# Matmuls on constants in the places where the program's own clock sees TensorE wait

## The chip, the cores and the metric

The kernel runs on one core of one Trainium2 chip. The metric is the device time of one execution in microseconds (us). TensorE (PE) multiplies into PSUM, where VectorE (DVE) and ScalarE (ACT) read the results; GpSimd (POOL) splits weights and issues some DMAs, and SyncE (SP) issues most of them. PEld is TensorE's loading of weights. The kernel uses PSUM as one tile of 8 banks of 512 fp32 values in each of 128 partitions.

## The reference, cut to what matters

Four layers in a row on a sequence of 2048 rows of 512 values, with 32 heads of 16 values: layer A (attention over all keys, with one key and value head for all 32 query heads), layer B (causal attention within four segments of 512 rows and a running memory beside it), then A and B again with the same weights. `phi(t)` is `t + 1` for positive `t`, else `exp(t)`.

```python
def _A_ref(x, wq, wk, wv, wo):            # H = 32, Dh = 16
    q = (x @ wq) by heads;  k = x @ wk;  v = x @ wv
    p = _softmax(einsum("bhqd,bkd->bhqk", q, k) * Dh ** -0.5)
    return einsum("bhqk,bkd->bhqd", p, v) by rows @ wo

def _B_ref(x, wq, wk, wv, wo, beta):      # N = 4 segments of L = 512
    for s in range(N):
        p = _softmax(qs @ ks.T * scale + mask)           # causal in the segment
        a_dot = p @ vs
        a_mem = (phi(qs) @ M) / (phi(qs) @ z + 1e-6)
        o = g * a_mem + (1.0 - g) * a_dot                # g = sigmoid(beta)
        M = M + phi(ks).T @ vs;  z = z + phi(ks) summed over rows
    return o @ wo

for layer in (A, B, A, B):
    x = x + layer(_layernorm(x, axis=-1))
```

## The kernel before

The rows are cut into four blocks of 512. A pair is one layer A and the layer B behind it; there are two pairs.

Layer A's attention (`a_scores`, `a_products`) runs unit by unit: a unit is four heads of one block, and each unit goes over 16 key tiles of 128. For a key tile TensorE writes two groups of eight small score matmuls (49 rows by 32 columns, written `bank<-qa,kst`, the first of a group at L99, the others at L102), ACT turns each group into exponentials `pa` (L751), and sixteen matmul halves multiply them by the values (`bank<-pa,va`). Scores live in pairs of PSUM banks, the ring `sc`; the exponentials live in nine buffers.

Everything else is the side work of a block (`side`): the output projection of A with the norm behind it (`out_norm`, `norm_tiles`: transposes at L514, `xh` and `xl`), the inputs of B (`b_inputs`: projections at L454, `qf`, `parts`, a bounce through DRAM by DMA, `sb<-parts` and `qkb<-sb`), the row maxima of its scores (`b_rowmax` with L988, in the last block `b_rowmax_masked` with L959), a transpose of the maxima (`guard_rows`, L687), its attention (`b_attend`, exponentials at L1027) and the output projection of B. These use single banks, the ring `r`: two of them (banks 4 and 5) beside layer A, six in the last part of the preparation, eight or four in the last block.

The order of the instructions is made when the program is built. The writer keeps a clock for each engine, `clk`, and adds an estimated cost for everything it emits: `pe(cost, form)` for TensorE, where `form` is how the array is split ("full", "rows" or "cols") and a change of form adds `DRAIN` = 130 ns; `on(engine, after, cost)` for the others. Each part of the work is a generator that yields the time at which its next piece can start (a bank of its ring free, its inputs there). `weave` runs the units of A beside the side work of one block, and `step` picks the generator whose next piece starts first; if that time lies ahead of `clk["pe"]`, the clock is set forward to it. There are eight phases, 0 to 7: phase 0 is laid beside the preparation, the others beside the side work of one block each. The side work of the very last block has no units beside it: `drive` runs it alone, from about 3000 us on. `together` issues a matmul that stays behind the one before it in TensorE's order.

`idb` is the identity and `maskq` a mask, both constants in SBUF (bf16).

Of the kernel before, what the change touches and what calls it, by code (L numbers as in the profile page):

```python
# [38 lines left out]
P = 128  # L39
S, D, H, DH = 2048, 512, 32, 16  # L40
NB, BT = 4, 512
# [48 lines left out]
def net_kernel(ctx, tc, x_in, a_wq, a_wk, a_wv, a_wo, b_wq, b_wk, b_wv, b_wo, b_beta, cst, out):  # L90
# [5 lines left out]
    def together(first, *a, **k):  # L96

        if first:
            nc.tensor.matmul(*a, **k)  # L99
        else:  # L100
            with tc.high_priority(offset=400):
                tc.keep_in_program_order(nc.tensor.matmul(*a, **k))  # L102
# [45 lines left out]
    def nm(s):  # L148
        uid[0] += 1
        return f"{s}_{uid[0]}"  # L150

    def st(shape, dt, tag):
        return one.tile(shape, dt, tag=tag, name=nm(tag))
# [15 lines left out]
    clk = {"pe": 0.0, "act": 0.0, "dve": 0.0, "pool": 0.0}  # L169
    evac_on = ["dve"]  # L170
    tiling = ["full"]

    def pe(cost, form="full"):
        clk["pe"] += cost + (DRAIN if form != tiling[0] else 0.0)
        tiling[0] = form
        return clk["pe"]
# [12 lines left out]
    def load_x(b):  # L189
        r = []  # L190
        for i in range(4):
            x_ = tmp(4, [P, 512], F32, "xt")
            nc.sync.dma_start(x_, x_in[b * BT + i * P:b * BT + (i + 1) * P, :])
            r.append(x_)
        return r
# [9 lines left out]
    maskq = st([P, 512], BF16, "maskq")  # L205
# [3 lines left out]
    idb = st([P, P], BF16, "idb")  # L209
# [89 lines left out]
    def wget(kind, n, ahead=2):  # L299

        wprefetch(n)
        r = []
        for j in range(n):
            k, i, w = wq_["ready"].pop(0)
            assert k == kind, (k, kind)
            r.append(w)
        wprefetch(ahead)
        return r
# [48 lines left out]
    rings = {}  # L357

    def layout(kind):

        n = clk["pe"]
        sc, r = {"a": (3, ()), "ab": (2, (4, 5)), "b": (2, (4, 5, 6, 7)), "b0": (0, (4, 5, 6, 7, 0, 1, 2, 3)), "z": (0, (4, 5, 6, 7, 0, 1, 2, 3)), "prep": (0, (0, 1, 2, 3, 4, 5)), "pa": (2, (4, 5))}[kind]
        for k, v in (("sc", pair_[:sc]), ("r", [one_[i] for i in r])):
            rings[k] = Ring(v)
            rings[k].free = [n] * len(v)

    def drive(gen):
        for rdy in gen:
            clk["pe"] = max(clk["pe"], rdy())

    class Need:
# [11 lines left out]
    def form_of(need):  # L383
        return need.form() if isinstance(need, Need) else "full"
# [25 lines left out]
    def step(zs, cost):  # L410

        now = clk["pe"]
        best = None
        for z in zs:
            if z[1] is None:
                continue
            at = z[1]()
            s = max(now, at) + (2 * DRAIN if form_of(z[1]) != tiling[0] else 0.0) + cost(z)
            if best is None or s < best[0]:
                best = s, at, z  # L420
        s, at, z = best
        assert at < 1e17
        clk["pe"] = t0 = max(now, at)
        z[1] = next(z[0], None)
        return z, clk["pe"] - t0

# [12 lines left out]
    def finish(za, until):  # L439
        while not until() and any(z[1] is not None for z in za):  # L440
            step(za, lambda z: PVL if z is za[1] else 0.0)
# [185 lines left out]
    def a_layer(i, exact):  # L627
        qmx = tmp(2, [32, 2 * NB], F32, "qmx")
        V.memset(qmx, 0.0)
        return {"exact": exact, "kst": kst[i], "va": va[i], "kr": [1e18] * NB, "qr": [[1e18] * 4 for _ in range(NB)],  # L630
                "sd": [dram.tile([H, 48, 512] if exact else [H, 33, 512], BF16 if exact else F16, tag=nm("sd"), name=nm("sd")) for _ in range(NB)],
                "kmx": tmp(2, [P, NB], F32, "kmx"), "qmx": qmx, "part": {}, "old": {}, "nq": 0}
# [131 lines left out]
    def a_products(n):  # L764

        for _ in range(n):
            yield Need(lambda: max(queue[0][-1], pva_free[0] if queue[0][1] else 0.0) if queue else 1e18, "rows")
            a_pv(*queue.pop(0))
# [372 lines left out]
    def everything(exact):  # L1141
        xs = [x_in] + [dram.tile([S, D], F32, tag=nm("x"), name=nm("x")) for _ in range(3)] + [out]
        L = a_layer(0, exact)

        spare = [x.rearrange("p j c -> p (j c)") for x in qa]
        spare = [x.bitcast(F32R).rearrange("p (a c) -> p a c", a=2) for x in spare]
        wq_["todo"] += ([("Akv", 0)] if exact else []) + [("Aq", t) for t in range(4)]
        for pair in range(2):
            for b in range(NB):
                ws = [("Ao", t) for t in range(4)] + [("Bv", t) for t in range(4)]  # L1150
                for t in range(4):
                    ws += [("Bq", t), ("Bk", t)]
                ws += [("Bo", t) for t in range(4)]
                if pair == 1 and b >= NB - 2:
                    end = b == NB - 1
                    ws = [(k, t, spare[t] if end and k == "Bv" and t < 2 else None, "take" if end else "keep") for k, t in ws]
                wq_["todo"] += ws
                if pair == 0:
                    wq_["todo"] += [("Akv", 0)] + [("Aq", t) for t in range(4)]
        aw = wget("Akv", 1) + wget("Aq", 4, 0)  # L1160
        layout("prep")
        evac_on[0] = "act"

        def prep(bs):
            bs = list(bs)
            if 0 in bs:
                ahead[0] = load_x(0) if exact else x_0, None
            for b in bs:
                xt, st_ = ahead.pop(b)
                for tiles in ((0, 1), (2, 3)) if st_ is None else ((0, 1, 2, 3),):  # L1170
                    yield from norm_tiles(xt, tiles, clk["pe"] + LOAD, st_)
                if b < NB - 1:
                    xt = load_x(b + 1)
                    ahead[b + 1] = xt, norm_stats(xt, (0, 1, 2, 3), clk["pe"] + LOAD)
                yield from a_prep(L, b, aw, b == 0 and not exact)
                evac_on[0] = "dve"

        ahead = {}

        def units(f, L, *parts):  # L1180
            return [(L, f, b, n, k0, k1) for b, k0, k1 in parts for n in range(8)]

        def side(b, pair, L, last=False):
            yield from out_norm(ota, 0, "Ao", xs[2 * pair], xs[2 * pair + 1], b, True, True)
            yield from b_block(b, last, exact, not exact and pair == 0 and b == 0)
            if last:
                layout("z")
            yield from out_norm(otb, 1, "Bo", xs[2 * pair + 1], xs[2 * pair + 2], b, pair == 0, False)
            if pair == 0:
                yield from a_prep(L, b, None)  # L1190

        if exact:
            drive(prep(range(NB)))
            layout("ab")
            for pair in range(2):
                LN = a_layer(1, exact)
                for b in range(NB):
                    drive(par(a_scores(units(0, L, (b, 0, 16))), a_products(128)))
                    drive(side(b, pair, LN))
                L = LN  # L1200
            return

        zb = prep(range(NB))
        while L["qr"][0][0] > 1e17:
            clk["pe"] = max(clk["pe"], next(zb)())
        layout("pa")
        LN = a_layer(1, exact)
        plan = [units(0, L, (0, 0, 4), (0, 4, 16))]
        plan += [units(f, L, (f, 0, 16)) for f in range(1, 4)]
        plan += [units(4, LN, (0, 0, 12), (1, 0, KA), (0, 12, 16)), units(5, LN, (1, KA, 16))]  # L1210
        plan += [units(f, LN, (f - 4, 0, 16)) for f in range(6, 8)]
        size = [sum(u[5] - u[4] for u in q) for q in plan]
        gone.clear()
        za = [[g, next(g)] for g in (a_scores(sum(plan, [])), a_products(sum(size)))]
        for f in range(8):
            phase[0] = f
            ta = (size[f] - gone.get(f, 0) - (32 if f == 4 else 0)) * 1500.0
            if f == 0:
                weave(za, TA0, zb, 55e3)
            else:  # L1220
                layout("ab")
                weave(za, TAF * ta, side((f - 1) % 4, (f - 1) // 4, LN), 150e3 if f < 5 else 133e3)
            layout("a")
            finish(za, lambda: gone.get(f, 0) == size[f])
            if f == 3:
                a_range(L)
        a_range(LN)
        layout("b0")
        evac_on[0] = "act"
        drive(side(NB - 1, 1, None, True))  # L1230
        assert not wq_["ready"] and not wq_["todo"]

    everything(False)
# [44 lines left out]
```

## Time and profile before

| | |
|---|---|
| median of 3 runs | 3179.75 us (3176.38 to 3182.36) |
| the profiled execution | 3173.99 us |
| its span, first to last instruction | 3172.1 us |
| mean granted TensorE clock in it | 0.975 of full |
| instructions | 116270 |

Times in the profile count from the start of the span. An engine's busy time is given in us and as a share of the span. A row of a group of instructions reads: line, engine, operation, tiles written and read, rows and columns of the array, shape, count, then busy us and mean ns of one, then the idle time just before them and what ended it. A row of a wait reads: who, for whom, us in total, times, longest. A row of the timeline reads: start, us, engine, line, and in brackets the idle time before it and its releaser. A row of the critical chain reads: start, us, engine, line. A row of a stretch has its bounds and length, the busy time of PE, PEld, DVE, ACT and POOL with instruction counts, the granted clock of TensorE (1.00 is full speed), the share of the DMA engines and GB/s.

### The profile page before, as it was taken

The numbers are of one execution on the slowest core, as the hardware profiler recorded it, in microseconds if no ns is written. First come the engines' busy times: TensorE is split into PE (matmuls) and PEld (weight loads), VectorE is DVE, ScalarE is ACT, GpSimd is POOL, SyncE is SP. The second block draws the span as 40 slices with busy tenths as digits, with TensorE's granted clock in tenths as the row PEclk, the third lists the DMA queues.
The fourth block names the chain that finished last, engine by engine and source line by source line (L and its number), as shares of the span: only waits on it lengthen the run. The fifth ranks groups of instructions, "written<-read, shape, count | busy, mean of one in ns | idle before, by whom it ended". The sixth has DMA issues, their size and how long they took to land.

```text
span 3172.1 us, 116270 instructions
## 1 busy us (share of the span) xinstructions
PE 2799.0 (88%) x51714; PEld 1329.8 (42%) x51714; DVE 1656.8 (52%) x4599; ACT 2325.2 (73%) x2583; POOL 396.0 (12%) x569
## 2 busy tenths in 40 slices
PE   6988898899888998889998898988998889988987
PEld 4533344345333454434443343443443334433544
DVE  7621355545655456556465454565445535555465
ACT  4699787876778767787778768668687876878523
POOL 2100010012100121002110020210110003100011
PEclk9999999999999999999999999999999999999978
DMA  4310121012210132102221132311221104311331
GB/s 124 99 42 22 46 63 43 25 50 78 67 39 18 54 91 58 35 15 73 89 63 46 33 108 66 92 47 34 84 63 31 48 12 160 95 48 33 114 106 34
DMA packets 138560, 194.11 MB, mean 61 GB/s; under 512 B 29664, under 2 KB 97088, under 8 KB 138048
## 3 DMA queue, kind: packets, MB, share of 16 engines
q1 hardware_dynamic: 118912, 121.56, 13.1%
q0 software_dynamic: 19136, 65.02, 7.2%
q8 instruction: 407, 6.67, 0.9%
q14 instruction: 105, 0.86, 0.1%
HBM read 126.46 MB, written 60.03 MB: 59 GB/s over the span
## 4 chain that ended last, share of the span: by engine, by line
PE 38%; ACT 31%; issue 15%; DVE 10%; DMA 3%; POOL 2%; SPq 0%; DVEq 0%; ACTq 0%; POOLq 0%
ACT pa L751 28%; PE bank L99 16%; PE bank L454 13%; PE bank L102 7%; DVE mo L988 4%; ACT pa L1027 3%; DVE m L959 1%; POOL w L186 1%; POOL parts L550 1%; DMA xt<-in_A_x_dram 1%; DMA wst<-in_B_wk_dram 1%; PE bank L514 1%; DMA wst<-in_B_wq_dram 1%; DVE parts L552 0%; DVE qf L532 0%
## 5 line engine op out<-in xcount | busy, mean ns | idle before, releaser
L751 ACT ACTIVATE pa<-bank 128x1024 f32<-128x1024 f32 x2048 | 1945.1, 1113 | 470.0 <-PE bank L102 465.5
L102 PE MATMUL bank<-pa,va 64*17 64x512 f32 x14336 | 1107.4, 601 | 0.2 <-DVE t L790 0.2
L99 PE MATMUL bank<-pa,va 64*17 64x512 f32 x2048 | 1065.5, 601 | 15.8 <-DVE ts L789 9.2
L99 PE MATMUL bank<-qa,kst 49*32 49x512 f16 x2048 | 746.1, 383 | 179.4 <-ACT pa L751 150.3
L102 PE MATMUL bank<-qa,kst 49*32 49x512 f16 x14336 | 827.9, 388 | 0.6 <-DVE xt L835 0.6
L988 DVE CUSTOM_DVE_ANT_0 mo<-bank,maskq 128x256 bf16<-128x256 f32 (+3 forms) x896 | 437.9, 489 | 209.5 <-PE bank L102 145.0
L102 PEld LDWEIGHTS <-kst 49*32 49x32 f16 x14336 | 227.5, 90 | 509.5 <-issue 498.7
L99 PE MATMUL bank<-qkb 48*32 48x128 f16 (+7 forms) x1536 | 346.4, 311 | 104.4 <-DVE m L988 46.0
L1027 ACT ACTIVATE pa<-bank 128x1024 f32<-128x1024 f32 (+2 forms) x384 | 323.7, 887 | 127.5 <-PE bank L102 125.1
L102 PE MATMUL bank<-qkb 48*32 48x384 f16 (+7 forms) x6656 | 369.9, 313 | 0.0
L99 PEld LDWEIGHTS <-kst 49*32 49x32 f16 x2048 | 174.3, 92 | 364.9 <-issue 340.3
L454 PE MATMUL bank<-xh,w 128*128 128x512 f32 x832 | 286.7, 409 | 11.6 <-DVE w L318 4.8
L102 PEld LDWEIGHTS bank<-pa,va 64*17 64x17 f32 x14336 | 259.4, 95 | 24.7 <-DVE t L790 8.8
L186 POOL TENSOR_SCALAR w<-wst 128x512 fp32r<-128x512 f32 x160 | 108.4, 679 | 1189.5 <-PE bank L454 1033.3
L454 PE MATMUL bank<-w,xh 128*128 128x512 f32 x752 | 246.7, 408 | 2.5 <-DVE xh L825 1.1
L102 PEld LDWEIGHTS <-qkb 48*32 48x32 f16 (+1 forms) x6656 | 152.8, 94 | 211.6 <-issue 202.6
L99 PEld LDWEIGHTS bank<-pa,va 64*17 64x17 f32 x2048 | 186.7, 94 | 105.7 <-DVE ts L789 14.5
L789 DVE STREAM_TRANSPOSE ts<-bank 128x512 f32<-128x512 f32 x88 | 62.8, 714 | 279.1 <-PE bank L102 278.9
L99 PEld LDWEIGHTS <-qkb 48*32 48x32 f16 (+1 forms) x1536 | 130.1, 96 | 155.0 <-issue 124.5
L454 PEld LDWEIGHTS bank<-xh,w 128*128 128x128 f32 x832 | 158.7, 191 | 80.0 <-issue 30.9
L1038 DVE STREAM_TRANSPOSE t<-bank 128x512 f32<-128x512 f32 x64 | 45.8, 715 | 273.6 <-PE bank L102 273.6
L102 PE MATMUL bank<-pa,vb 128*17 128x384 f32 (+3 forms) x1920 | 171.4, 442 | 8.5 <-ACT pa L1027 7.6
(164 smaller groups left out, 2987.5 us busy)
## 6 DMA issues: line engine op xcount, KB each, us to landing
sb<-parts SPq DMA_DIRECT2D x128, 128.0 KB
qkb<-sb SPq DMA_DIRECT2D x256, 64.0 KB
x<-xt SPq DMA_DIRECT2D x48, 256.0 KB
xt<-x SPq DMA_DIRECT2D x48, 256.0 KB
qa<-sd SPq DMA_DIRECT2D x176, 66.0 KB
wd<-w POOLq DMA_DIRECT2D x20, 512.0 KB, 3.7
w<-wd POOLq DMA_DIRECT2D x18, 512.0 KB, 6.1
xt<-in_A_x_dram SPq DMA_DIRECT2D x32, 256.0 KB
```

The source lines that it names most:

```text
L99: nc.tensor.matmul(*a, **k)
L102: tc.keep_in_program_order(nc.tensor.matmul(*a, **k))
L186: G.tensor_scalar(o, i, 1.0, 0.0, op0=ALU.mult, op1=ALU.add)
L454: T.matmul(ps, lhsT=l_(kt), rhs=r_(kt), start=n == 0, stop=n == 11)
L514: T.transpose(ps[:, k, :], xn[:, k * P:(k + 1) * P], ident)
L550: G.tensor_scalar(parts[:, 0, :], x, up, 0.0, op0=ALU.mult, op1=ALU.add)
L751: A.activation(x, sc, AF.Exp, scale=scale)
L789: V.transpose(ts.rearrange("p a b -> p (a b)"), pva[:, 0, :])
L959: V.reduce_max(m[:, u0:u0 + per, i, qt], ps[:, 0:per * nk].rearrange("p (h k) -> p h k", k=nk), axis=AX.X)
L988: V.tensor_tensor_reduce(out=mo[:, 0:nk], in0=ps[:, o_:o_ + nk], in1=maskq[:, 512 - nk:512], op0=ALU.add, op1=ALU.max, scale=1.0, scalar=- ...
L1027: A.activation(e[:, :, 0:w], sc[:, :, 0:w], AF.Exp, scale=0.25 if exact else 0.25 / (UPB * UPB))
L1038: V.transpose(t1.rearrange("p a b -> p (a b)"), pvb)
```

## The change

`fill(until)` is new. Where `step` would set TensorE's clock forward to `at`, and, in the side work of the last block, before each yielded time, it writes matmuls on constants: identity (`idb`) against `maskq`, into the bank of the ring `r` that was freed first. It does so only while more than 400 ns of the wait are left, less than 0.7 of the last 3400 ns on TensorE's clock is booked as work, and a bank of the ring is free by the clock. A matmul has up to 512 moving columns; it uses all 128 columns of the array if the current form is "full", and 32 of them otherwise. What they write is never read. `busy` is the list of booked work for that share. The matmuls count on `clk["pe"]` with their cost and with `DRAIN`, so the choices of `step` after them can differ too.

```diff
+    SPAN = 3400.0
+    DUTY = 0.7
+    busy = []
+
+    def duty():
+        while busy and busy[0][1] < clk["pe"] - SPAN:
+            busy.pop(0)
+        return sum(b - max(a, clk["pe"] - SPAN) for a, b in busy) / SPAN
+
+    def fill(until):
+
+        ring = rings["r"] if rings["r"].slots else None
+        while ring and until - clk["pe"] > 400.0 and duty() < DUTY and min(ring.free) < clk["pe"]:
+            i = min(range(len(ring.free)), key=lambda j: ring.free[j])
+            rows, cols_ = (P, P) if tiling[0] == "full" else (P, 32)
+            n = int(min(512, max(128, (until - clk["pe"] - 260.0) * 2.4))) // 64 * 64
+            together(False, ring.slots[i][0:cols_, 0:n], lhsT=idb[0:rows, 0:cols_], rhs=maskq[0:rows, 0:n], start=True, stop=True)
+            pe(n / 2.4, "cols" if cols_ == 32 else "full")
+
     def pe(cost, form="full"):
+        busy.append((clk["pe"], clk["pe"] + cost))
...
-    def drive(gen):
+    def drive(gen, warm=False):
         for rdy in gen:
+            if warm:
+                fill(rdy())
             clk["pe"] = max(clk["pe"], rdy())
...
         s, at, z = best
         assert at < 1e17
-        clk["pe"] = t0 = max(now, at)
+        fill(at)
+        clk["pe"] = t0 = max(clk["pe"], at)
         z[1] = next(z[0], None)
         return z, clk["pe"] - t0
...
-        drive(side(NB - 1, 1, None, True))
+        drive(side(NB - 1, 1, None, True), True)
```

In the changed program the lines behind the new functions have moved: L454 is L477, L514 is L537, L687 is L710; `together` keeps L99 and L102. The program gets 171 such matmuls, each with a load of `idb`: 133 in the phases, 38 in the last block. All other instructions are the same ones, but many stand in another order.

The first place is TensorE in phase 1 (about 464 us): the last scores of one group of eight and the first of the next. Before:

```order
L102 LDWEIGHTS kst_21_121
L102 MATMUL bank<-qa_26_130,kst_21_121 32x512
L99 LDWEIGHTS kst_21_121
L99 MATMUL bank<-qa_26_130,kst_21_121 32x512
L102 LDWEIGHTS kst_21_121
L102 MATMUL bank<-qa_26_130,kst_21_121 32x512
```

and now:

```order
L102 LDWEIGHTS kst_21_121
L102 MATMUL bank<-qa_26_130,kst_21_121 32x512
L102 LDWEIGHTS idb_97
L102 MATMUL bank<-maskq_95,idb_97 32x512
L99 LDWEIGHTS kst_21_121
L99 MATMUL bank<-qa_26_130,kst_21_121 32x512
```

One filler of 128 rows by 32 columns has come between two groups of scores; nothing else moved here.

The second place is TensorE in the last block, between the transpose of the first unit's maxima (`m`) and the first scores of the second unit, whose queries and keys are `qkb_28`. Before:

```order
L102 LDWEIGHTS idb_97
L102 MATMUL bank<-maskw_106,idb_97 32x128
L687 MATMUL bank<-cs_89,m_52850 16x128
L99 LDWEIGHTS qkb_28_132
L99 MATMUL bank<-qkb_28_132 32x512
```

and now, of six equal fillers the first:

```order
L102 LDWEIGHTS idb_97
L102 MATMUL bank<-maskw_106,idb_97 32x128
L710 MATMUL bank<-cs_89,m_52997 16x128
L102 LDWEIGHTS idb_97
L102 MATMUL bank<-maskq_95,idb_97 128x512
```

Six full fillers now stand behind the transpose and ahead of the first scores of the second unit.

The third place is TensorE a little earlier in the last block, at the transposes of the norm's third and fourth tile (`xn`). Before:

```order
L454 MATMUL bank<-w_52691,xl_157 128x512
L514 MATMUL bank<-cs_89,xn_52745 128x128 x4
L514 MATMUL bank<-cs_89,xn_52773 128x128 x4
L454 MATMUL bank<-qa_25_129,xh_156 128x512 x2
L454 MATMUL bank<-xh_156,w_52693 128x512
```

and now, behind the third tile's transposes:

```order
L477 MATMUL bank<-w_52824,xh_156 128x512 x2
L477 MATMUL bank<-w_52824,xl_157 128x512
L537 MATMUL bank<-cs_89,xn_52884 128x128 x4
L102 LDWEIGHTS idb_97
L102 MATMUL bank<-maskq_95,idb_97 128x512
```

Eight full fillers have come between the third tile's transposes and the fourth's (`xn_52912`), which ran one behind the other.

## The prediction

> **What bounds the kernel now.** I read the busy shares first, then the waits of TensorE (PE) and ScalarE (ACT), then the clock by stretch, then the last block row by row.
>
> ```profile
> PE 2799.0 (88%) x51714; PEld 1329.8 (42%) x51714; DVE 1656.8 (52%) x4599; ACT 2325.2 (73%) x2583; POOL 396.0 (12%) x569
> PE 38%; ACT 31%; issue 15%; DVE 10%; DMA 3%; POOL 2%; SPq 0%; DVEq 0%; ACTq 0%; POOLq 0%
> L99 PE MATMUL bank<-qa,kst 49*32 49x512 f16 x2048 | 746.1, 383 | 179.4 <-ACT pa L751 150.3 <-ACT pa L1027 9.3 <-DVE qmx L599 0.4
> ...
> 27.20:3000.00 2972.80, 2647.57 (x49103) 1240.69 (x49101) 1537.01 (x4295) 2269.19 (x2509) 359.33 (x505) 0.98 0.21 59
> 3000.00:3172.10 172.10, 141.31 (x2582) 81.30 (x2582) 100.09 (x242) 51.50 (x68) 25.42 (x40) 0.82 0.28 86
> ```
>
> PE is busy 88% of the span, ACT 73%, and the chain that ended last changes between them: neither covers the other. The two stretches (us, then busy time of PE, PEld, DVE, ACT, POOL, then granted clock) say what a lower clock can cost at most: in the eight interleaved phases and before, to 3000, 0.02 x 2973 = 59 us, in the last block alone 0.18 x 172 = 31 us.
>
> ```profile
> PE bank L99 <- ACT pa L751: 168.0, 451, 5.0
> PE bank L99 <- DVE m L988: 46.0, 100, 2.4
> ...
> ACT pa L751 <- PE bank L102: 465.5, 298, 10.8
> ```
>
> PE really waits for a score bank 451 times, 0.37 us each (168.0 / 451), which is 22% of the 2048 score groups that L99 begins. ACT starves for scores 298 times.
>
> **The filler in the phases.** By the instruction order 133 fillers are added there, 128 rows by 32 columns, with 61,888 moving columns in all (121 times 512), in 110 places, two thirds of them straight ahead of a score group. They stand where the bookkeeping's clock waits, not the chip's. The price of one is bounded by the nearest rows, a lone 128-row matmul between products and scores:
>
> ```profile
> 506.73 0.59 PE L99 MATMUL bank<-pa,va 64*17 64x512 f32 x1
> 506.73 0.61 PE L102 MATMUL bank<-pa,va 64*17 64x512 f32 x7
> 507.27 0.23 PE L893 MATMUL bank<-sqq,ones 128*32 128x128 bf16 x1
> 507.43 0.39 PE L99 MATMUL bank<-qa,kst 49*32 49x512 f16 x1
> ...
> 507.65 0.59 PE L99 MATMUL bank<-pa,va 64*17 64x512 f32 x1
> ...
> 508.08 0.59 PE L99 MATMUL bank<-pa,va 64*17 64x512 f32 x1
> ...
> 508.51 0.38 PE L99 MATMUL bank<-qa,kst 49*32 49x512 f16 x1
> ```
>
> From the second half of a product to the next score it takes 508.51 - 508.08 = 0.43 us without it and 507.43 - 506.73 = 0.70 us with it: 0.27 us. Scores of 512 columns go by in 507.65 - 507.43 = 0.22 us, so its 128 columns stream for 0.06 us and 0.21 us is the change of tiling. All fillers: 121 x 0.22 + 110 x 0.21 = 27 + 23 = 50 us, if none lies in a real wait; 0, if all do. I take neither end. If the bookkeeping picks real waits no better than chance, 22% of 50 us, or 11, is covered on the spot. The other 39 us delays PE; what follows is either a PE wait on ACT, which swallows it, or an ACT starved by PE, which does not: 298 of 298 + 451 is 40%. A wait swallows 0.37 us and a filler with its switches costs 50 / 110 = 0.45, so I take 45%: 18 us on the path. Fillers may also stand behind DVE, since a bank is written that DVE has read; 19 of the 110 places get a wait of their own. The nearest row is 46.0 / 100 = 0.46 us: 0 to 9 us. I take 0, because an idle bank is looked for, and keep 9 for the range. The other rows that move (on ACT about 130 of 2500 stand in another order) I price at 0, between -5 and +5.
>
> **The clock in the phases.** Windows of 3.4 us (same columns as above):
>
> ```profile
> 1617.80:1621.20 3.40, 2.62 (x84) 1.03 (x79) 2.93 (x8) 3.38 (x5) 0.00 (x0) 1.00 0.01 1
> 1621.20:1624.60 3.40, 3.40 (x61) 1.54 (x64) 1.71 (x7) 2.23 (x3) 0.00 (x0) 0.50 0.23 83
> 2792.00:2795.40 3.40, 2.17 (x30) 0.49 (x25) 3.37 (x7) 3.40 (x5) 1.14 (x2) 1.00 0.53 162
> 2795.40:2798.80 3.40, 3.40 (x33) 0.73 (x33) 2.28 (x6) 0.04 (x1) 0.00 (x0) 0.50 0.23 72
> ```
>
> A window with PE busy for 2.2 to 2.6 of 3.4 us is followed by one at half clock, though no idle stretch fills it. One costs at most half of 3.4, 1.7 us. A filler adds 0.22 of 3.4 us, 6%, and of the 59 / 1.7, at most 35, such windows before 3000 I find only six whose cause, the window ahead, holds a filler or has one just before it. I take one of them avoided: -2 us, with 0 and -10 (six) as ends. The Trainium skill ("TensorE: Matmul & The Clock Gate", section "HAM oscillation — how this bites in real kernels") states that the clock falls after PE idles for more than about 3.4 us. The trace disagrees: 2.62 us of work did not hold it. By that rule the clock terms, here and below, would be nil.
>
> **The last block.** It gets 38 fillers: 6 and 8 full ones (128 columns) among the transposes of the norm, 6 full ones after the first row of maxima, 18 narrow ones later.
>
> ```profile
> 3006.96 1.04 PE L514 MATMUL bank<-cs,xn 128*128 128x128 f32 x8
> 3008.28 0.73 PE L454 MATMUL bank<-qa,xh 128*128 128x512 f32 x2 [0.29 <-ACT xh L517]
> ...
> 3024.78 0.40 PE L454 MATMUL bank<-xh,w 128*128 128x512 f32 x1
> 3032.11 0.58 PE L99 MATMUL bank<-qkb 48*32 48x512 f16 x1 [6.94 <-DMA sb<-parts]
> ...
> 3039.74 0.38 PE L687 MATMUL bank<-cs,m 128*16 128x128 f32 x1 [2.81 <-DVE m L959]
> 3040.16 0.58 PE L99 MATMUL bank<-qkb 48*32 48x512 f16 x1
> ...
> 3024.10:3027.52 3.42, 1.07 (x5) 0.56 (x3) 1.29 (x2) 0.66 (x2) 1.18 (x2) 1.00 0.94 320
> 3027.52:3032.10 4.58, 0.00 (x0) 0.02 (x1) 0.00 (x0) 0.00 (x0) 0.00 (x0) 0.50 0.85 266
> 3032.10:3045.40 13.30, 10.01 (x257) 6.93 (x258) 12.01 (x26) 0.00 (x0) 0.00 (x0) 0.50 0.26 69
> 3045.40:3058.23 12.83, 12.56 (x285) 6.18 (x288) 9.03 (x20) 6.11 (x7) 0.00 (x0) 0.50 0.17 44
> ...
> 3041.61 5.64 DVE L959 TENSOR_REDUCE m<-bank 128x1 f32<-128x512 f32 x11
> ...
> 3105.97 1.45 PE bank L102 x27
> ...
> 3121.13 2.34 PE bank L102 x27
> ...
> 3134.36 2.55 PE bank L102 x27
> ```
>
> The eight stand between the third and fourth transposes, which ran without a gap: 8 x 0.22 = 1.8 us later for the norm's last tile, with 0.29 us of slack behind it, hence for the projection, the bounce through DRAM and the row of maxima at 3032. The six ahead of them are partly under a wait: +2 us together (0 to 3). The one long gap, 6.94 us for the DMA, gets no filler, so the fall to half clock at 3027.5 stays. The six at 3040 follow L687 and hold up the next maxima, on which DVE is already waiting: at half clock 6 x 0.44 = 2.6 us. Against that they fill most of a window, and I expect full clock from about 3046 instead of 3058. DVE carries 3032 to 3045 (12.01 of 13.30 busy); PE carries 3045 to 3058 (12.56 of 12.83), and DVE needs 9.03 there, so 12.83 us can shrink by 4 at most: -4 + 2.6 = -1.4 (from +2.6 to -4). The four next narrow ones cost 0.6 (0 to 1.5). The later pairs lie near DVE and ACT waits, so I cost them at nothing. If that cover is gone, what comes late is the scores behind them. They fall in or near three windows before half-clock stretches. A group of 27 takes 1.45 us at full clock and 2.34 or 2.55 at half, so each stretch avoided saves about 1.0; half of three, -1.2. Sum of the block: 2 - 1.4 + 0.6 - 1.2 = 0.
>
> **Sum.** 18 - 2 + 0 = +16 us. The profiled execution took 3173.99 us (span 3172.1 and 1.9 around it), so 3190 in its terms. It lies 5.8 us under the median of the three runs, 3179.75, to which the forecast refers: 3195, rounded down a little. About 0.2% (6 us) is what a measurement of this kernel can tell from no change.
>
> **The rivals.** (a) *The waits are real.* The fillers in the phases cost nothing and the clock moves little: the 18 falls to 0 or 4, giving 3178 to 3184. For it: 168 us of waits exist. Against it: PE is busy 89% there (2647.57 of 2972.80). This is also the case where the change does little.
> (b) *Faster: the clock in the last block.* If full clock returns at 3046 and the three later stretches vanish, the block gains 4 + 3 - 2.6 = 4 us with its first term hidden; if the fillers of the phases also sit in real waits and save the six windows (-10), the time is 3180 - 14 = 3166. It decides at whether six full matmuls restore the clock by 3046. Against it: PE was busy throughout 3045 to 3058 and the clock stayed at 0.50.
> (c) *All unhidden.* 50 us, 9 us behind DVE, nothing from the clock: 3225 to 3238.
> (d) *The clock does not care for fillers outside long idle gaps.* Then -2, -4 and -1.2 drop out: 3195 + 7 = 3202. The skill's rule named above would give this one.
>
> **How the numbers follow.** Forecast and its neighbourhood, 3187 to 3200: 0.40; (a) 0.27; (b) 0.15; (c) 0.08; (d) 0.10. The range 3172 to 3216 leaves out most of (b) and (c). Slower by over 0.2% is the forecast, (c) and (d): 0.58. Same is (a): 0.27. Faster is (b): 0.15.
>
> **What would show it.** PE's busy time grows by about 30 to 50 us and ACT's stays; the waits L99 <- ACT fall by some 20 to 30 us while ACT's idle time before L751 grows; the mean clock to 3000 stays at 0.98; in the last block 6.94 us before the first maxima stay and full clock comes back before 3058. The forecast is wrong if PE's waits shrink by as much as its busy time grows (a), or if the clock of the last block rises above 0.9 (b).

## The result, and the profile after

The changed kernel takes 3206.64 us (median of 4 runs, 3204.27 to 3220.31), the kernel before 3178.07 us beside it (4 runs, 3172.34 to 3182.36). The ratio, taken over all these runs, is 1.0098, 95% interval 1.0075 to 1.0121: 31 us more (24 to 38); the two medians lie 28.6 us apart. The forecast was 3195 us, between 3172 and 3216, and "slower" as the likeliest outcome. The profiled execution took 3204.27 us, with a span of 3202.4 us, 30.3 longer than that of before.

The page of the kernel after: busy time of the engines, then shares of the chain that ended last.

```profile
PE 2835.0 (89%) x51883; PEld 1352.0 (42%) x51885; DVE 1655.1 (52%) x4599; ACT 2329.5 (73%) x2583; POOL 396.9 (12%) x569
PE 36%; ACT 28%; issue 18%; DVE 10%; DMA 4%; POOL 3%; SPq 0%; DVEq 0%; ACTq 0%; POOLq 0%
```

PE is busy 36.0 us longer than before (2799.0), its weight loading (PEld) 22.2 us longer (1329.8 before); DVE, ACT and POOL are busy as long as before within 5 us. "Issue", time in which an engine waited for nothing that the profile shows, has grown on the chain from 15% to 18%, and PE and ACT have shrunk from 38% and 31%. The fillers by shape (groups of PE's matmuls) and the waits, whose first lines answer to those of before:

```profile
L102 PE MATMUL bank<-maskq,idb 128*32 128x512 bf16 x96 | 36.4, 402 | 0.0
...
L102 PE MATMUL bank<-maskq,idb 128*128 128x512 bf16 x18 | 6.6, 520 | 0.3 <-issue 0.2
```

```profile
PE bank L99 <- ACT pa L774: 149.5, 410, 4.8
PE bank L99 <- DVE m L1011: 52.9, 103, 5.3
...
PE bank L99 <- DVE ts L812: 13.0, 10, 3.3
...
ACT pa L774 <- PE bank L102: 501.7, 319, 10.8
```

PE's wait for exponentials has fallen by 18.5 us (168.0 to 149.5), as the fillers meant it to. But ACT's wait for scores has grown by 36 (465.5 to 501.7), and two single waits of PE have become longer: 5.3 us for the maxima `m` (2.4 before) and 3.3 us for `ts`, the transposed result of a unit of layer A (1.7 before). Both come from DVE.

Stretches of the kernel after, then of before, from 27 us to the last product of the phases, and from there to the end (us, busy time of PE, PEld, DVE, ACT, POOL, granted clock, DMA share, GB/s):

```profile
27.20:3001.09 2973.89, 2659.76 (x49172) 1249.08 (x49172) 1520.41 (x4257) 2272.97 (x2508) 356.43 (x497) 0.98 0.20 58
3001.09:3202.40 201.31, 166.12 (x2682) 96.00 (x2684) 114.88 (x279) 51.83 (x68) 29.65 (x48) 0.84 0.30 92
```

```profile
27.20:2982.45 2955.25, 2631.06 (x49034) 1228.14 (x49032) 1521.74 (x4255) 2268.95 (x2508) 355.02 (x497) 0.98 0.20 58
2982.45:3172.10 189.65, 157.82 (x2653) 93.85 (x2652) 115.37 (x280) 51.74 (x68) 29.73 (x48) 0.83 0.32 100
```

The phases have become 18.6 us longer, the last block 11.7. The clock is 0.98 in the phases both times, and 0.84 instead of 0.83 in the block: over the whole kernel it explains nothing. In the two places shown below it is lower than before.

I cut the phases apart at the end of the last `bank<-pa,va` matmul of each, in the timeline, and take lengths from it. Differences to before (us), in one profiled execution each; the experiments follow below.

| kernel | phase 1 | phase 7 | the six others | last block |
|---|---|---|---|---|
| length before | 382.0 | 363.0 | 2237.4 | 189.7 |
| after | +11.8 | +9.8 | -2.9 | +11.7 |
| e1 fillers in the phases | +10.3 | +10.0 | +2.1 | +1.1 |
| e2 fillers in the last block | -1.4 | +0.6 | -4.4 | +5.8 |
| e3 booked, not written | +9.1 | +14.7 | -2.7 | +4.7 |
| e4 written, not booked | -1.3 | -0.6 | +3.7 | +11.1 |
| e5 as e3, splits on GpSimd | +8.2 | +20.9 | +12.3 | +2.0 |
| e6 before, splits on GpSimd | -1.1 | +3.5 | +9.9 | +2.8 |
| e8 before, `DRAIN` 131 | +9.2 | +5.9 | +9.1 | +1.7 |
| e9 phases 0, 2 to 5 | -2.3 | +0.8 | -0.4 | +1.0 |
| e10 phase 1 alone | +9.6 | -3.1 | -1.5 | +0.3 |
| e12 phases 6 and 7 | -0.1 | +10.0 | +0.8 | +3.8 |

One execution scatters by some us in each column: runs that keep before's order in phase 1 or 7 (e7 and e11 too, cut in the same way) read between -3.1 and +3.5 there. So the verdicts below go by several runs of each kernel. But where a run has the changed kernel's order, the pattern is plain: phases 1 and 7 pay about 10 us each, the other six together nothing. In e5, e6 and e8 the other six are 9 to 12 us longer as well.

### The profile page after: what moved, and what is told of

It is laid out like the page before. It is cut to its first block, busy times and chain, and to the rows that moved or that the text cites. A ratio compares the mean times of both kernels' runs of the same rounds, so it can differ in the third digit from the quotient of the medians.

```text
span 3202.4 us, 116560 instructions
## 1 busy us (share of the span) xinstructions
PE 2835.0 (89%) x51883; PEld 1352.0 (42%) x51885; DVE 1655.1 (52%) x4599; ACT 2329.5 (73%) x2583; POOL 396.9 (12%) x569
## 4 chain that ended last, share of the span: by engine, by line
PE 36%; ACT 28%; issue 18%; DVE 10%; DMA 4%; POOL 3%; SPq 0%; DVEq 0%; ACTq 0%; POOLq 0%
ACT pa L774 25%; PE bank L99 15%; PE bank L477 12%; PE bank L102 7%; DVE mo L1011 4%; ACT pa L1050 3%; DVE m L982 1%; POOL w L206 1%; DMA wst<-in_B_wq_dram 1%; DMA wst<-in_B_wk_dram 1%; POOL parts L573 1%; PE bank L537 1%; DMA wst<-in_B_wv_dram 1%; DVE parts L575 0%; DMA sb<-parts 0%
## 5 line engine op out<-in xcount | busy, mean ns | idle before, releaser
L774 ACT ACTIVATE pa<-bank 128x1024 f32<-128x1024 f32 x2048 | 1945.6, 1113 | 507.0 <-PE bank L102 501.7
L102 PE MATMUL bank<-pa,va 64*17 64x512 f32 x14336 | 1103.1, 600 | 0.2 <-DVE t L813 0.2
L99 PE MATMUL bank<-pa,va 64*17 64x512 f32 x2048 | 1062.9, 599 | 18.5 <-DVE ts L812 13.0
L99 PE MATMUL bank<-qa,kst 49*32 49x512 f16 x2048 | 743.7, 382 | 167.9 <-ACT pa L774 134.7
L102 PE MATMUL bank<-qa,kst 49*32 49x512 f16 x14336 | 825.1, 387 | 0.6 <-DVE xt L858 0.6
L99 PE MATMUL bank<-qkb 48*32 48x512 f16 (+7 forms) x1536 | 346.7, 307 | 110.8 <-DVE m L1011 52.9
L102 PEld LDWEIGHTS <-kst 49*32 49x32 f16 x14336 | 228.0, 90 | 500.3 <-issue 488.1
L102 PE MATMUL bank<-qkb 48*32 48x384 f16 (+7 forms) x6656 | 369.4, 310 | 0.7 <-issue 0.4
L99 PEld LDWEIGHTS <-kst 49*32 49x32 f16 x2048 | 173.4, 92 | 357.3 <-issue 334.8
L477 PE MATMUL bank<-xh,w 128*128 128x512 f32 x832 | 286.2, 408 | 14.6 <-DVE w L338 5.0
L102 PEld LDWEIGHTS bank<-pa,va 64*17 64x17 f32 x14336 | 256.3, 95 | 25.7 <-DVE t L813 11.1
L477 PE MATMUL bank<-w,xh 128*128 128x512 f32 x752 | 246.5, 408 | 4.6 <-DVE xh L848 1.0
L102 PEld LDWEIGHTS <-qkb 48*32 48x32 f16 (+1 forms) x6656 | 151.6, 93 | 219.0 <-issue 209.6
L99 PEld LDWEIGHTS bank<-pa,va 64*17 64x17 f32 x2048 | 185.6, 94 | 114.9 <-DVE ts L812 19.4
L99 PEld LDWEIGHTS <-qkb 48*32 48x32 f16 (+1 forms) x1536 | 129.4, 94 | 152.8 <-issue 114.1
L477 PEld LDWEIGHTS bank<-xh,w 128*128 128x128 f32 x832 | 158.4, 191 | 81.7 <-issue 32.9
L308 DVE TENSOR_TENSOR w<-wst,w 128x512 fp32r<-128x512 f32 x160 | 115.6, 725 | 112.9 <-POOL w L206 111.9
```

The lines of the kernel that those rows point to most:

```text
L308: V.tensor_tensor(w[:, 1, :], s, f(w[:, 0, :]), op=ALU.subtract)
L477: T.matmul(ps, lhsT=l_(kt), rhs=r_(kt), start=n == 0, stop=n == 11)
L774: A.activation(x, sc, AF.Exp, scale=scale)
```

## The experiments

Each time stands beside runs of the kernel before on the same chip; intervals are those of the ratio.

**e1 to e4: which half of the change costs.** The change has two effects: matmuls are written, and their cost is booked on the program's clock, which moves other instructions. e1 and e2 part the places, e3 and e4 the effects.

e1 leaves out the last block's fillers:

```diff
-        drive(side(NB - 1, 1, None, True), True)
+        drive(side(NB - 1, 1, None, True))
```

> Fillers in the phases alone (133), none in the last block. The changed kernel ended the phases 18.6 us later than before and lost another 11.6 us in the last block. If the two add up: +18.6 us, ratio 1.006. If the late start of the last block brought its loss by itself: +30 us, ratio 1.0095. If the phases cost nothing by themselves: within 0.2% of before.

Measured: 3196.59 us, 1.0066 (1.0051 to 1.0080), so +21 us (16 to 25).

e2 leaves out those of the phases:

```diff
-        fill(at)
         clk["pe"] = t0 = max(clk["pe"], at)
```

> Fillers in the last block alone (38). Theory, they delay a chain and give no clock back: +11 to +12 us, ratio 1.0035 to 1.004. Rival, the block's loss came from the phases' other alignment with the clock's windows: within 3 us of before, with the half-clock stretch of 30.7 us ended early.

Measured: 3183.19 us, 1.0022 (1.0009 to 1.0035), +7 us (3 to 11), between the two answers expected. With e1 that makes 28 of the 31 us.

e3 books the fillers and does not write them, so it has the changed kernel's order without its added work (on ACT instruction for instruction, on DVE but for some 2% of them):

```diff
-            together(False, ring.slots[i][0:cols_, 0:n], lhsT=idb[0:rows, 0:cols_], rhs=maskq[0:rows, 0:n], start=True, stop=True)
             pe(n / 2.4, "cols" if cols_ == 32 else "full")
```

> The fillers are booked on the program's clock but not written: the order of the changed kernel without a filler in it. Theory, the fillers' own time on TensorE is what costs: within 5 us of before (ratio 0.9985 to 1.0015). Rival, the other order of the real instructions costs: +15 to +25 us, ratio 1.005 to 1.008.

Measured: 3201.76 us, 1.0081 (1.0065 to 1.0097), +26 us (21 to 31).

e4 writes 168 fillers and puts the clock back behind them, so that before's choices stay:

```diff
+        was = clk["pe"], tiling[0], list(busy)
...
+        clk["pe"], tiling[0] = was[0:2]
+        busy[:] = was[2]
```

> The fillers (168) are written but not booked: the order of before on ACT, with fillers in it. Theory, the fillers' own time costs: +25 to +32 us, ratio 1.008 to 1.010. Rival, the order costs: under +15 us, ratio under 1.005.

Measured: 3185.39 us, 1.0035 (1.0023 to 1.0048), +11 us (7 to 15).

The order alone, with no matmul added, costs most of the loss (e3 has the changed order in the last block too; e1, with order and fillers of the phases, cost 21). The fillers in the old order cost 11 us, of which the last block takes 7 by e2.

**e11: what a filler in the phases costs.** e4's fillers in the phases alone (127), each written twice, not booked:

```diff
-            together(False, ring.slots[i][0:cols_, 0:n], lhsT=idb[0:rows, 0:cols_], rhs=maskq[0:rows, 0:n], start=True, stop=True)
+            for _ in range(2):
+                together(False, ring.slots[i][0:cols_, 0:n], lhsT=idb[0:rows, 0:cols_], rhs=maskq[0:rows, 0:n], start=True, stop=True)
```

> Fillers in the phases alone, in before's order (written, not booked), each written twice: 254 instead of 127, none in the last block. With fillers once in before's order in phases and last block the time was 3185.4, with the last block's alone 3183.2, so once costs about 2 us in the phases. Theory (they lie in stretches in which TensorE would wait anyway, and take its waits): twice costs 3 to 8 us, 3180 to 3185. Rival (the prediction's step: 45% of the uncovered streaming is on the path, +18 for once): 40 us for twice, 3210 to 3220.

Measured: 3180.03 us, 1.0009 (0.9997 to 1.0020): +3 us (-1 to +6) for 254 of them. The page of e11, and PE's wait for exponentials in it:

```profile
PE 2841.4 (89%) x51968; PEld 1346.0 (42%) x51968; DVE 1660.6 (52%) x4599; ACT 2329.6 (73%) x2583; POOL 398.8 (13%) x569
...
PE bank L99 <- ACT pa L778: 146.1, 398, 5.4
```

PE is busy 42 us longer than before and the time does not follow; its wait for exponentials is 21.9 us shorter (168.0 before). So in the old order the fillers go into PE's waits, on the spot or a little later, which this run does not tell apart; the price of one on the path is 3 / 254, about 0.01 us, and at most 6.4 / 254 = 0.025.

**e9, e10, e12: where the order costs.** `fill` returns at once outside the phases named:

```diff
-        ring = rings["r"] if rings["r"].slots else None
+        ring = rings["r"] if rings["r"].slots and phase[0] in (6, 7) else None
```

e9 has the change in phases 0 and 2 to 5 (71 fillers), e10 in phase 1 (27), e12 in 6 and 7 (36); the edit shown is e12's, and none of the three has fillers in the last block. On ACT, e9 and e12 have before's order in all phases left out, and e12 has after's from phase 6 on; e9's phases 2 and 3 have an order of their own, since phase 1 ahead of them is before's.

> The change (fillers written and booked) in phases 0 and 2 to 5 alone: 71 of its 168 fillers; phases 1, 6, 7 and the last block stand in before's order, without fillers. Theory (the moved order costs at two places, near 685 us in phase 1 and near 2720 us in phase 7, and nothing elsewhere): no loss, 3170 to 3179, since these five phases together were 5.5 us shorter in the changed kernel's profile. Rival (any move away from before's order costs its share, and each filler its 0.2 us): 71 of the 133 fillers of the phases, so some 10 to 16 us more than before, 3187 to 3193.

Measured: 3175.12 us, 0.9997 (0.9986 to 1.0009). 71 fillers and the moves of five phases cost nothing that can be told from no change.

> The change in phase 1 alone: 27 fillers, and the order of phase 1 as the changed kernel has it; all other phases and the last block as before. Theory (one place, near 685 us, where the transposes of a unit stand behind the side work's chain on VectorE): phase 1 is 8 to 12 us longer and the time 3185 to 3190. Rival (loss spread over all moves): 27 of 133, so +4 at most, 3178 to 3182, and phase 1 less than 5 us longer.

Measured: 3188.62 us, 1.0039 (1.0024 to 1.0054), +12 us (8 to 17).

> The change in phases 6 and 7 alone: 36 fillers, and from there on the order of the changed kernel; phases 0 to 5 stand in before's order, and the last block has no fillers. Theory (the second of two places, near 2720 us, where loads of weights and their splits stand in the queues ahead of what TensorE needs next): phase 7 is 8 to 15 us longer, the time 3186 to 3193, and with the 12 us of phase 1 alone this adds up to the 19 to 24 us of all phases. Rival (what is left is spread over the phases 0 and 2 to 6 and shows only together): phase 7 less than 5 us longer, 3177 to 3182.

Measured: 3193.03 us, 1.0059 (1.0039 to 1.0079), +19 us (12 to 25).

Both answers are those of two bad places. Their prices do not simply add up: 12 + 19 = 31 us, where e1, which has both, cost 21 (16 to 25); the intervals leave room for either. What happens at the first is seen in DVE's timeline (start, us, engine, line), of before and then of after:

```profile
676.93 0.72 DVE L789 STREAM_TRANSPOSE ts<-bank 128x512 f32<-128x512 f32 x1 [1.01 <-PE bank L102]
...
679.94 1.09 DVE L288 TENSOR_TENSOR w<-wst,w 128x512 fp32r<-128x512 f32 x1 [1.22 <-POOL w L186]
...
681.12 0.62 DVE L835 TENSOR_TENSOR xt<-xt,bank 128x512 f32<-128x512 f32 x1
```

```profile
682.09 0.68 DVE L858 TENSOR_TENSOR xt<-xt,bank 128x512 f32<-128x512 f32 x1
...
686.43 0.69 DVE L308 TENSOR_TENSOR w<-wst,w 128x512 fp32r<-128x512 f32 x1 [1.71 <-POOL w L206]
687.04 0.71 DVE L812 STREAM_TRANSPOSE ts<-bank 128x512 f32<-128x512 f32 x1
```

`ts` empties the bank of a finished unit. Before, it stands ahead of the side work's evacuation `xt` and of the second halves of the weights `w`. Now it stands behind both, and the last `w` waits for a load. The chain of work that ended last, of after, runs through it (start, us, what):

```profile
680.33 1.07 POOL w L206
681.40 4.24 DMA wst<-in_A_wq_dram
...
685.79 0.62 POOL w L206
686.43 0.26 DVE w L308
...
687.04 0.72 DVE ts L812
...
687.81 1.89 PE bank L99 x2
...
695.66 1.02 ACT pa L774
```

PE waits 3.3 us there for `ts` (its row of the waits above). A stretch of before behind its `ts`, then the stretches of after around the wait, in columns as above:

```profile
683.00:690.00 7.00, 6.48 (x136) 2.84 (x135) 4.53 (x18) 7.00 (x8) 0.54 (x1) 1.00 0.42 143
...
680.00:687.40 7.40, 3.87 (x56) 1.67 (x54) 4.65 (x12) 3.77 (x4) 3.88 (x6) 1.00 0.42 115
687.40:694.20 6.80, 6.39 (x45) 1.95 (x53) 3.24 (x13) 1.02 (x1) 1.29 (x3) 0.50 0.31 77
```

PE does 3.87 us of work in 7.40, then catches up at half clock, and ACT has 1.02 us of work in 6.80 until the next scores come at about 695. From the load to there the chain needs some 15 us, and the phase is 10 to 12 us longer. Of that, half clock for 6.80 us can be at most 3.4; it begins as the wait for `ts` ends, not ahead of it.

The second place, in phase 7: a stretch of 55 us with the side work's projections of queries and keys, PE's longest waits in it and DVE's wait for weights, of before and then of after.

```profile
2685.00:2740.00 55.00, 50.90 (x863) 25.62 (x870) 33.70 (x84) 42.99 (x49) 18.90 (x28) 0.98 0.50 158
...
PE bank L99 <- ACT pa L751: 3.0, 7, 1.0
PE bank L99 <- DVE m L988: 0.4, 1, 0.4
...
DVE w L288 <- POOL w L186: 4.1, 2, 2.3
```

```profile
2695.00:2750.00 55.00, 43.31 (x651) 20.64 (x643) 24.55 (x62) 34.32 (x38) 15.15 (x24) 0.88 0.45 138
...
PE bank L99 <- DVE m L1011: 5.3, 1, 5.3
PE bank L99 <- DVE pk L937: 4.6, 1, 4.6
...
DVE w L308 <- POOL w L206: 17.3, 4, 7.1
```

And DVE's timeline of after at that place:

```profile
2719.58 0.69 DVE L308 TENSOR_TENSOR w<-wst,w 128x512 fp32r<-128x512 f32 x1 [6.89 <-POOL w L206]
2721.10 0.69 DVE L308 TENSOR_TENSOR w<-wst,w 128x512 fp32r<-128x512 f32 x1 [0.83 <-POOL w L206]
2721.71 0.68 DVE L937 COPY pk<-bank 128x512 f32<-128x512 f32 x1
2729.53 0.69 DVE L308 TENSOR_TENSOR w<-wst,w 128x512 fp32r<-128x512 f32 x1 [7.13 <-POOL w L206]
2730.14 0.69 DVE L1011 CUSTOM_DVE_ANT_0 mo<-bank,maskq 128x512 bf16<-128x512 f32 x1
```

DVE stands idle for 6.89 and 7.13 us at the head of its queue, because the first half of a weight on POOL waits for the load. Behind it stand `pk`, which empties a bank of transposed keys, and `mo`, whose maxima are `m`; PE needs both at once, and they run the moment the `w` is done. Before, DVE waited for such weights twice there, 2.3 us at the longest, and ACT was busy 42.99 of the 55 us instead of 34.32. The clock is 0.88 there instead of 0.98, at most 0.10 x 55 = 5.5 us of the 10. e12 shows the same two rows in PE's waits:

```profile
PE bank L99 <- DVE pk L937: 4.6, 1, 4.6
PE bank L99 <- DVE m L1011: 4.4, 1, 4.4
```

**e5 and e6: is it the split of the weights?** My first theory for both places was the `w` at the head of DVE's queue. e5 is e3 with these subtractions on GpSimd, e6 is before with them:

```diff
-        V.tensor_tensor(w[:, 1, :], s, f(w[:, 0, :]), op=ALU.subtract)
+        (G if parts == "keep" or kind == "Aq" else V).tensor_tensor(w[:, 1, :], s, f(w[:, 0, :]), op=ALU.subtract)
```

> The changed kernel's order without its filler matmuls (booked on the program's clock, not written), and the second step of the weight split (the subtraction that writes the low half of w) on GpSimd instead of VectorE, for the query weights and for the loads of the last side work. Theory (a split that waits for GpSimd and a DMA stands in VectorE's in-order queue ahead of work that TensorE needs): the stretches near 685 and near 2720 us lose their stalls, phases 1 and 7 come back to within 3 us of before's, and the time falls from 3201.8 to 3178 to 3186. Rival (the loss is the order on TensorE and ScalarE themselves, the split only happens to stand there): phases 1 and 7 stay 8 to 14 us longer than before's and the time stays at 3198 to 3204.

Measured: 3207.42 us, 1.0090 (1.0076 to 1.0105), +29 us (24 to 33).

> The kernel before with the same subtractions on GpSimd, as a control. Theory of the queue: before waits only 4.1 us on VectorE for GpSimd there and TensorE not at all, so the move gives nothing: 3174 to 3181. Rival: the move is worth something by itself (then what it gives to the changed order says nothing): under 3170. Against: GpSimd's subtraction holds up the next weights: above 3184.

Measured: 3190.14 us, 1.0041 (1.0027 to 1.0054), +13 us, spread over phases that have no bad place. The groups on POOL, of e6, give the reason for a part of it:

```profile
L288 POOL TENSOR_TENSOR w<-wst,w 128x512 fp32r<-128x512 f32 x40 | 53.7, 1343 | 2.5
```

A subtraction takes 1.34 us there (on DVE 0.73, as 160 of them took 116.5 us before), in the queue that also issues the loads. So for phase 7 e5 decides nothing; nor do the prices add up, 26 (e3) and 13 being more than e5's 29. For phase 1 it does: the `w` is gone from DVE's queue, and the place still costs 8.2 us. DVE and PE in e5's timeline:

```profile
683.72 0.69 DVE L857 TENSOR_TENSOR xt<-xt,bank 128x512 f32<-128x512 f32 x1 [4.39 <-PE bank L476]
...
687.82 0.71 DVE L811 STREAM_TRANSPOSE ts<-bank 128x512 f32<-128x512 f32 x1
...
688.59 1.89 PE L99 MATMUL bank<-pa,va 64*17 64x512 f32 x2 [2.03 <-DVE ts L811]
```

`ts` now waits behind `xt` and the eleven small steps of the norm that follow it, and PE waits 2.03 us, where it is 2.4 in e3 and 3.3 in the changed kernel. For phase 1 my theory in its narrow form falls: the split is what DVE happens to wait on. What the runs share is that the unit's `ts` stands behind the side work's chain.

**e8: is it this change's order, or any other?** No filler; one number of the bookkeeping, by which 55 of ACT's instructions stand elsewhere:

```diff
-    DRAIN = 130.0
+    DRAIN = 131.0
```

> The kernel before with one number of the bookkeeping changed (the drain of a matmul, 130 to 131 ns): 55 of ScalarE's instructions and 2270 of TensorE's stand in other places; no filler. Theory (any other order costs, since this one was picked among many): 3185 to 3205, with a stall of VectorE's weight split or the like in some phase. Rival (most orders are as good, and the changed kernel met one bad place in each of two phases): 3174 to 3184.

Measured: 3200.25 us, 1.0068 (1.0055 to 1.0082), +22 us (17 to 26). The theory holds in its number, and not quite in its words, since e9 moves 5 phases for nothing. In phase 1, e8 takes the same turn as the changed kernel: the same wait for `ts` (2.3 us) in the same place, +9.2 us. One nanosecond in a cost is enough to fall into it. The rest of its loss lies elsewhere: in phase 7 (+5.9) PE's longest wait near the second place is 5.1 us for the DMA `qkb<-sb`, not for `pk` or `m`, and the 9.1 us of the other six phases are not explained.

**e7: the clock in the last block.** 30 full fillers in the one long gap there, the 6.94 us for the DMA, in the kernel before:

```diff
+                    if n == 0 and qt == 3 and i == 0 and u0 == 0:
+                        for _ in range(30):
+                            together(False, ps, lhsT=idb, rhs=maskq, start=True, stop=True)
```

> The kernel before with 30 matmuls of 128x128x512 on the identity written ahead of the first row maxima of the last block, where TensorE waits 6.94 us for a DMA. At 0.22 us each they take 6.5 us, inside the wait. Theory (the clock of the last block falls with TensorE's idle and comes back with streaming): full clock from there on for one or two windows, 2 to 6 us off the last block, 3172 to 3176. Rival (the clock falls again at once in the thin row-tiled work behind it): 3177 to 3180, half clock in the last block still 55 to 65 us. If the wait ends early they cost up to 3 us: 3181.

Measured: 3170.72 us (12 runs), 0.9988 (0.9975 to 1.0002): not to be told from no change, at most 8 us gained. The median lies under both answers expected. The profiled execution is the slowest of the twelve (3181.75 us; eight took 3166 to 3175), so it says nothing sure of the faster ones. The fillers in e7's timeline, and two stretches behind them:

```profile
3033.01 6.42 PE L102 MATMUL bank<-maskq,idb 128*128 128x512 bf16 x29
...
3034.00:3042.10 8.10, 6.65 (x71) 2.94 (x71) 1.70 (x3) 0.00 (x0) 0.61 (x1) 1.00 0.73 231
3042.10:3062.58 20.48, 17.35 (x483) 10.99 (x468) 17.86 (x41) 5.00 (x6) 0.00 (x0) 0.50 0.18 48
```

They fit the gap (the first maxima then wait 1.16 us) and hold the full clock through it, where before fell to half. At 3042 it falls all the same, and the last block of this execution is 189.4 us long, 0.3 less than before. In this execution nothing is lost or won there: DVE carries the stretch, busy 17.86 of its 20.48 us.

No version measured is faster than the kernel before by more than can be told from no change.

## Why the prediction was right, and where it was not

The direction, the range and the outward signs were right: PE's busy time (+36.0, forecast 30 to 50), ACT's longer waits, the clock of 0.98, the gap before the first maxima (7.6 us). The wait for ACT fell by a little less than forecast (18.5, not 20 to 30). But the size was off, 31 us instead of 16, and the cause of most of the loss was not the one that I gave.

- **The filler in the phases: +18 forecast, nothing that can be told measured.** The failing number is the 45% of the uncovered streaming that should reach the path, and ahead of it the 22% that a wait covers. The 22% took the bookkeeping's waits as no better than chance, the 45% let nearly half of the rest delay the kernel. e11 shows that the fillers find waits: 254 of them cost 3 us (-1 to +6). Rival (a) was right on this term, in before's order; in the changed order, after and e3 differ by 5 us for all fillers, the last block's included.
- **The other rows that move: 0 forecast, between -5 and +5; +26 measured** (e3, 21 to 31, with the last block's order in it; by e1 the phases cost 21, 16 to 25, fillers included). This is the step that failed. I counted ACT's moved rows and priced them as noise around zero. But in before's order no evacuation at the two places stood long behind a weight that waits for its load, and in the changed order some do. Every kernel whose order differs in one of these phases lost in it (phase 1: 8.2 to 11.8 us in after, e1, e3, e5, e8, e10; phase 7: 5.9 to 14.7 us in after, e1, e3, e8, e12). These are not as many independent orders: there, all but e8 have the changed kernel's, exactly or nearly. And the order of five other phases moved for nothing (e9). The rows of DVE and not of ACT would have shown the first place: `ts` behind `xt` and `w` can be read from the order.
- **Behind DVE: 0 forecast, 9 as the end.** As a price of the fillers' own waits, nothing in e11 speaks for more than 0.
- **The clock in the phases: -2 forecast.** 0.98 before and after; 2 us are too small to be seen or excluded. No gain from the clock was seen anywhere, as in rival (d), but its reason does not hold: the long stretch at half clock in the last block lasts 17.1 us in after, e2 and e4, which have fillers there, and 23.9 to 30.7 in before and in every other run. The rule of the Trainium skill that I set beside it ("TensorE: Matmul & The Clock Gate", section "HAM oscillation — how this bites in real kernels") names idle time of more than about 3.4 us; e7 fell to half clock without it, right behind a stretch with PE busy 6.65 of 8.10 us, so idle for 1.45 in all.
- **The last block: 0 forecast; +7 measured alone (e2, 3 to 11), +11.7 in the changed kernel's profile.** The fillers' streaming was sized well. The timeline of after shows the eight among the transposes of the norm and five of the six behind the first maxima:

```profile
3027.55 0.60 PE L537 MATMUL bank<-cs,xn 128*128 128x128 f32 x4
3027.99 1.89 PE L102 MATMUL bank<-maskq,idb 128*128 128x512 bf16 x8
3029.71 0.49 PE L537 MATMUL bank<-cs,xn 128*128 128x128 f32 x3
...
3062.14 0.38 PE L710 MATMUL bank<-cs,m 128*16 128x128 f32 x1 [2.81 <-DVE m L982]
3062.74 2.34 PE L102 MATMUL bank<-maskq,idb 128*128 128x512 bf16 x5 [0.22 <-issue]
3065.02 0.61 PE L99 MATMUL bank<-qkb 48*32 48x512 f16 x1
```

  The eight hold up the next transposes by 1.72 us (3029.71 - 3027.99; forecast 1.8), and with the six ahead of them the last of these comes 3.7 us later than the end of the phases explains (in e2 1.9; forecast 2). From one transpose of maxima to the next (L687, L710) it takes 3.7 us longer than before, in after and e2 alike (forecast 2.6). What failed is the clock's -4: full clock did come back, 4.5 us behind that transpose instead of 18.5, and fell again after one window. The kernel after:

```profile
3066.60:3070.00 3.40, 1.87 (x92) 1.19 (x77) 3.40 (x7) 0.00 (x0) 0.00 (x0) 0.99 0.19 47
3069.95:3073.36 3.41, 3.14 (x34) 0.94 (x34) 2.05 (x5) 1.18 (x2) 0.00 (x0) 0.50 0.07 19
```

  In the one full window DVE is the bound (3.40 of 3.40 us busy), so nothing was gained in it. Whether the -1.2 for later stretches came cannot be told from the block's mean clock, 0.83 before and 0.84 after.

In sum, what was put at 18 for the fillers, 0 for the order and 0 for the last block came out near 0, 21 to 26 and 7. That the time fell into the range was luck: a cost that was not there made up for most of one that was not counted.

A slip in the rivals: (c) by its own terms begins at 3180 + 50 = 3230 us, not 3225; nothing hangs on it.

What stays open: in phase 1 no run puts `ts` alone back ahead of the side work's chain, so that this is the cause is read from the rows and from the runs with and without that order. How much of each place is the wait and how much the half clock behind it was not parted. The 10 us of phase 7 are placed there by e12, and its rows show `pk` and `mo` behind weights that wait for loads, but no run takes that wait away cleanly, since e5's move costs something by itself. In the last block, e3 and e12, without fillers there, are 4.7 and 3.8 us longer in one execution each; whether this is the order or scatter was not settled.

## What to carry to other kernels

Where the writer's cost model sets the order, any edit to its clock is also an edit to the order, and the two can be priced apart: write the work without booking it, and book it without writing it. Before pricing moved rows at zero, compare the order on the engine that empties the banks, and look for an evacuation that has slipped behind an instruction that waits for a load; a place where that was seen cost about 10 us here. The writer's clock cannot see such a place: it books the second half of a weight as `on("dve", 0.0, 602)`, which waits for no load. Filler work in waits was free on TensorE, but it bought nothing either: in the one window of the last block where it brought full clock back, DVE was the bound.

## What the hardware showed that I had not expected

254 fillers, in pairs in 127 places of the old order, add 42 us to PE's busy time and 3 us (-1 to +6) to the kernel's: a filler between products and scores, for which I had read 0.21 us of switching from the timeline, costs nothing that can be told where the bookkeeping sees a wait, even on an engine that is busy 89% of the phases.

The clock is half behind busy windows too: in the last block of e7 it stays at 0.50 for 20.48 us in which PE is busy 17.35, after 8.10 us at full clock with PE busy 6.65.
